# A fixed bound in place of a measured one: the second softmax's deviation set to 2^-10, its largest-|x| reductions left out, and a running minimum added

## The chip, the cores and the metric

One core of a Trainium2 chip runs the kernel. The metric is device time in microseconds (us), the median over runs; the profile is one execution on the same core. The engines are PE (matrix multiplies; PEld is its weight load), VectorE (DVE), ScalarE (ACT), GpSimd (POOL) and SyncE (SP), whose queue issues all data transfers here.

## The reference

For each of 4 batches x is 12480 tokens of 128 channels; 32 inducing vectors are shared. An attention step makes 32 rows h, a second one mixes them for every token, and a two-layer MLP with a squared ReLU follows.

```python
def mab(q, kv):
    s = scale * (q @ kv.transpose(0, 2, 1))
    s = s - s.max(-1, keepdims=True)
    a = np.exp(s)
    a /= a.sum(-1, keepdims=True) + 1e-09
    return a @ kv
h = mab(I, x)                  # I: inducing, 32 rows
y = mab(x, h)                  # every token against the 32 rows of h
...
r = np.maximum(y @ w_in, 0.0)  # d_ff = 2048
out = (r * r) @ w_out
```

## The kernel before

The second softmax is nearly flat: each of a token's 32 weights a lies close to 1/32. So y is close to the mean of the rows of h, and the sign of almost every hidden column of `y @ w_in` is the same for all tokens. If no weight falls short of 1/32 by more than a share rho, a column's smallest and largest possible value follow from the 32 numbers `h @ w_in` alone. Columns that are never positive are dropped (`dead`), columns that are always positive (`pos`) become a quadratic form in the deviations d = 2^14 (a - 1/32), and at most 16 others (`mix`) are computed singly. That needs 512 squared columns (`pairs`, `g`) instead of 2048.

The work is staged by batch. `first(b)` reads all x of a batch twice, transposed (`xp` tiles, 7 groups G of up to 1920 columns) and straight (`xnb` tiles, two per group): scores of the first softmax on PE, scaled and their maximum taken on VectorE (`sT`, L254), the bias `nb` (L287), exp on ScalarE (L300), a transpose (`en`, L310), the accumulation `hacc` on PE (L323) into `hq` (L331), and at the end the normalised, transposed h (`hn`, `hT`). `prepare(b)` makes the weights of the batch: `hwv` = h w_in (L448), the largest |value| spread over all partitions (`row`, `bc`, `p2`, named `p` in the profile), the scaled copy `hws` (L494), the column classes, the product `R` (L529), and 4 blocks of quadratic weights `G` (VectorE, L605), `wq` (PE, L611), `w` (L165). `second(b, G)` makes a group's weights a: scores (L236), transpose (L362), row maximum (L364), subtraction on GpSimd (L368), exp (L369), sum (L372), product with the reciprocal on GpSimd (L375), transpose back (L378), rounding to fp16 on ScalarE or VectorE (L385 or L387), the split-off rest (L388), and a transfer through DRAM that lays the deviations out for PE (`ad`, `dT`). `squares(b, G)` adds the single columns. A `Chunk` of 480 tokens then takes two `hp` products and squares (`up`, `lift`: L639, L648), five accumulations (`down`: L654, L655) and one evacuation `o`, on ScalarE (L658) or VectorE (L660).

The order of the program around the chunks is written out: `background(k)` gives, after every half chunk, so many steps of `second` of this and the next batch, of `first` and `prepare` of the next batch, and of `squares`. Batch 0's `first` and `prepare` run ahead of its chunks, mixed with the narrowing of the weights from 64-bit words (`ni`, `no`, L206 to L212). A scheduler then orders the instructions of each engine; every engine works through its own queue in order.

The bound rho is measured in before. `largest(G)` (L292) takes the largest |x| of each channel over an `xp` tile, one VectorE reduction of 1920 elements for each group (28 in all, tile `xm`). `prepare` multiplies these with the largest deviation of h's rows from their mean (`dh`, `ah`, L455 to L459; the matmul L474), scales the result (L477, L479), spreads it beside the largest value (L484, L501) and uses it as a per-partition operand. Each batch writes a flag: rho at most 2^-8, no more than 16 mixed columns, and a check of ranges. If one of the flags is 0, a branch behind the chunks computes all batches again with all 2048 columns (`every_column`).

Where an evacuation or a rounding may go to either engine, `to_act` decides by a ledger of planned time, `held`, which `largest` also writes to:

```python
if held["act"] + act < held["dve"] + dve:
    held["act"] += act
    return True
held["dve"] += dve
return False
```

Of the kernel before, what the change touches and what calls it, by code (L numbers as in the profile page):

```python
# [40 lines left out]
def attend_then_relu2_mlp(ctx: ExitStack, tc: tile.TileContext, xn, xT, indT, w_in, w_out, outT):  # L41
# [198 lines left out]
    def first(b):  # L240
# [49 lines left out]
        def largest(G):  # L290
            held["dve"] += 60 + 1.042 * 4 * WID[G]
            nc.vector.tensor_reduce(  # L292
                st.xm[:, G:G + 1], st.xp[G], axis=AX.X, op=ALU.max, apply_absolute_value=True,
            )

# [141 lines left out]
    def prepare(b):  # L437
# [37 lines left out]
        row = work.tile([1, 2], F32, tag="row", name=f"row_{b}")
        nc.vector.tensor_reduce(row[:, 0:1], ps[0:1, 0:P], axis=AX.X, op=ALU.max)
        nc.vector.tensor_reduce(row[:, 1:2], ps[0:1, P:P + MI], axis=AX.X, op=ALU.max)  # L477
        ts(row[:, 0:1], row[:, 0:1], 2.0 ** -60, None, op0=ALU.max)
        ts(row[:, 1:2], row[:, 1:2], 2 * scale * (1 + 2.0 ** -8), 2.0 ** -16, op0=ALU.mult, op1=ALU.add)  # L479
# [4 lines left out]
        nc.vector.tensor_copy(two, ps[:, 0:2])  # L484
# [2 lines left out]
        ts(p2.bitcast(I32), two[:, 0:1].bitcast(I32), 0x7F800000, None, op0=ALU.bitwise_and)
# [16 lines left out]
        ts(vm, v, omr, None, op0=ALU.mult)  # L504
# [435 lines left out]
```

## Time and profile before

| | |
|---|---|
| runs, median (lowest to highest) | 576.62 us (575.87 to 576.66) |
| the profiled execution, first to last instruction | 577.3 us; no time is listed for it beside this span |
| mean granted clock of PE | 0.869 |
| busy: PE, VectorE, ScalarE, GpSimd | 438.9, 365.3, 296.8, 83.4 us |
| transfers | 100.82 MB, mean 175 GB/s |
| first lift of batches 0, 1, 2, 3 | 100.3, 236.7, 360.8, 486.6 us |

A row of the profile's groups gives line, engine, operation, `out<-in` with shapes, the count, busy time and the mean of one in ns, and behind the second bar the engine's idle time just before these instructions with what ended it. The chain of waits is the work that ended last, followed backwards from the end: time outside it can be saved without shortening the run. In the lines by stretch, the numbers are the stretch, its length, the busy time of PE, PEld, VectorE, ScalarE and GpSimd with their counts, PE's granted clock, the share of the transfer engines and GB/s. In a waits row stand who waited, for whom, the total, the times and the longest.

### The profile page before, as it was taken

How to read it: one execution, taken by the hardware profiler on the slowest of the kernel's cores; microseconds unless marked ns; L12 is line 12 of the kernel's file. 1: busy time of each engine (PE TensorE's matmuls, PEld its weight loads, DVE VectorE, ACT ScalarE, POOL GpSimd, SP SyncE). 2: the span in 40 equal slices, each digit the busy share in tenths (PEclk: the TensorE clock that was granted, in tenths of full speed). 3: DMA queues.
4: the chain of work that ended last, by engine and by line, in shares of the span. 5: the costliest groups of instructions: out<-in, count | busy, mean ns of one | idle time of the engine just before them, and what ended most of it. 6: DMA issues, size and time to landing. Idle time of an engine off the chain costs nothing.

```text
span 577.3 us, 8820 instructions
## 1 busy us (share of the span) xinstructions
PE 438.9 (76%) x3083; PEld 204.5 (35%) x3083; DVE 365.3 (63%) x947; ACT 296.8 (51%) x419; POOL 83.4 (14%) x93
## 2 busy tenths in 40 slices
PE   1615465777798889769878899769777999897882
PEld 0014334522233536413333545313243555223330
DVE  6999758662555268997254298985534378767342
ACT  0030112437577266747875376628574476565771
POOL 0000011030211010242021021222011022422010
PEclk9999655997789569989889799969969599899997
DMA  8958715024528606565867535735866332334543
GB/s 322 399 214 277 277 69 154 1 86 155 179 80 305 199 20 226 172 182 167 280 226 230 178 102 186 270 104 145 311 211 190 107 105 72 97 126 130 168 132 131
DMA packets 64590, 100.82 MB, mean 175 GB/s; under 512 B 22800, under 2 KB 53776, under 8 KB 64528
## 3 DMA queue, kind: packets, MB, share of 16 engines
q1 hardware_dynamic: 64528, 100.08, 52.1%
q8 instruction: 28, 0.46, 0.3%
q14 instruction: 34, 0.28, 0.2%
HBM read 64.91 MB, written 31.95 MB: 168 GB/s over the span
## 4 chain that ended last, share of the span: by engine, by line
PE 44%; DVE 28%; ACT 13%; issue 6%; DMA 3%; POOL 3%; SPq 1%; POOLq 0%; ACTq 0%; DVEq 0%
PE po L654 10%; PE hp L639 9%; ACT g L648 8%; PE s L236 7%; DVE xm L292 5%; PE hwv L448 5%; PE hacc L323 4%; DVE G L605 3%; DMA outT_dram<-o 2%; PE po L655 2%; PE wq L611 2%; ACT o L658 2%; DVE e L362 2%; PE R L529 2%; DVE z L372 2%
## 5 line engine op out<-in xcount | busy, mean ns | idle before, releaser
L648 ACT ACTIVATE g<-hp 128x960 f16<-128x960 f32 x208 | 193.2, 970 | 87.9 <-PE hp L639 48.9
L639 PE MATMUL hp<-dT,pairs 96*128 96x480 f16 x416 | 122.0, 385 | 29.0 <-ACT g L648 28.1
L654 PE MATMUL po<-g,w 128*128 128x480 f16 x416 | 119.4, 399 | 16.1 <-ACT o L658 6.0
L368 POOL TENSOR_TENSOR e<-e,mx 128x480 f32<-128x480 f32 (+1 forms) x28 | 26.5, 947 | 334.8 <-DVE mx L364 222.8
L639 PEld LDWEIGHTS <-pairs 96*128 96x128 f16 x416 | 37.8, 99 | 97.6 <-issue 75.7
L654 PEld LDWEIGHTS <-w 128*128 128x128 f16 x416 | 41.1, 104 | 75.4 <-issue 43.9
L292 DVE TENSOR_REDUCE xm<-xp_False 128x1 f32<-128x1920 f32 (+1 forms) x28 | 55.7, 1989 | 5.3 <-DMA xp_False<-xT_dram 5.3
L658 ACT ACTIVATE o<-po,bias,osc 128x480 f32<-128x480 f32 x66 | 48.9, 753 | 18.9 <-PE po L655 7.1
L236 PE MATMUL s<-xp_False,indT_sb 128*32 128x480 f32 (+1 forms) x224 | 37.7, 743 | 20.5 <-DMA xp_False<-xT_dram 12.3
L323 PE MATMUL hacc<-xnb,en 128*32 128x128 f32 x784 | 39.2, 328 | 17.2 <-issue 9.3
L655 PE MATMUL po<-dT,lin 128*128 128x480 f16 x104 | 42.3, 408 | 2.7 <-DMA dT<-zz 2.7
L432 POOL TENSOR_TENSOR zz<-z 128x480 f16<-128x480 f32 (+1 forms) x28 | 28.9, 1030 | 87.8 <-DVE z L428 72.1
L660 DVE TENSOR_SCALAR o<-po,osc,bias 128x480 f32<-128x480 f32 x38 | 28.7, 767 | 18.0 <-DMA outT_dram<-o 6.8
L323 PEld LDWEIGHTS hacc<-xnb,en 128*32 128x32 f32 x784 | 26.7, 129 | 34.3 <-issue 20.1
L300 ACT ACTIVATE sT<-sT,nb 128x480 f32<-128x480 f32 (+1 forms) x28 | 18.2, 653 | 35.5 <-DVE nb L287 35.5
L236 PE MATMUL s<-xp_False,hT 128*32 128x480 f32 (+1 forms) x224 | 34.5, 628 | 2.1 <-DVE s L357 1.7
L375 POOL TENSOR_TENSOR e<-e,z 128x480 f32<-128x480 f32 (+1 forms) x28 | 27.6, 986 | 53.8 <-DVE z L374 48.6
L428 DVE TENSOR_SCALAR z<-sq,off,cut 128x480 f32<-128x480 f32 (+1 forms) x28 | 21.4, 764 | 21.8 <-PE sq L422 21.7
L605 DVE TENSOR_TENSOR G<-hwp,hw 128x512 f16<-128x512 f16 x64 | 30.1, 510 | 5.0 <-PE wq L611 4.7
L369 ACT ACTIVATE e<-e 128x480 f32<-128x480 f32 (+1 forms) x28 | 16.1, 574 | 31.6 <-POOL e L368 31.6
L362 DVE STREAM_TRANSPOSE e<-s 128x480 f32<-128x480 f32 (+1 forms) x28 | 18.0, 644 | 15.4 <-PE s L236 14.9
L331 DVE TENSOR_TENSOR hq<-hacc,hq 128x128 f32<-128x128 f32 x24 | 6.8, 284 | 33.0 <-PE hacc L323 33.0
(208 smaller groups left out, 498.6 us busy)
## 6 DMA issues: line engine op xcount, KB each, us to landing
outT_dram<-o SPq DMA_DIRECT2D x104, 240.0 KB, 2.2
xp_False<-xT_dram SPq DMA_DIRECT2D x24, 960.0 KB, 5.8
xnb<-xn_dram SPq DMA_DIRECT2D x28, 448.0 KB, 6.1
xnb<-xn_dram SPq DMA_DIRECT2D x24, 512.0 KB, 5.8
dT<-ad SPq DMA_DIRECT2D x72, 120.0 KB, 2.7
ad<-a SPq DMA_DIRECT2D x24, 240.0 KB, 2.7
dT<-zz SPq DMA_DIRECT2D x104, 30.0 KB, 1.9
wi<-w_in_dram SPq DMA_DIRECT2D x4, 512.0 KB, 5.4
```

Source lines behind the costliest of these rows:

```text
L236: nc.tensor.matmul(ps[32 * q:32 * q + 32, 0:w], lhsT, xp[:, w * q:w * q + w], start=True, stop=True,)
L292: nc.vector.tensor_reduce(st.xm[:, G:G + 1], st.xp[G], axis=AX.X, op=ALU.max, apply_absolute_value=True,)
L323: st.last = nc.tensor.matmul(hacc[32 * q:32 * q + 32, 0:P], en[:, t], xg[:, t % 8], start=t < 4, stop=t + 4 >= nb32,)
L362: nc.vector.transpose(ef[:, 0:wb], ps[:, 0:wb])
L432: nc.gpsimd.tensor_tensor(g[rows], zv[rows], zv[rows], op=ALU.mult)
L448: nc.tensor.matmul(ps[:, k * (MI + 1):(k + 1) * (MI + 1)], w_in_sb[:, f:f + P], st.hT[:, 96:P + 1], start=True, stop=True,)
L605: tt(g[:, :, MI * j:MI * j + n], hwp[:, :, 0:n], hw16f[:, :, s0:s0 + n], op=ALU.mult)
L639: nc.tensor.matmul(hp[:, i, 0:CH].rearrange("p (q t) -> p q t", q=4), pairs[0:96, (2 * j + i) * P:(2 * j + i + 1) * P], self.dT[0:96], sta ...
L648: nc.scalar.activation(self.g[:, 2 * j:2 * j + 2], self.hp.pop(j)[:, 0:2, 0:CH], AF.Square)
L654: nc.tensor.matmul(po[:, 0:CH], st.w16[:, i], self.g[:, i], start=i == 0, stop=False)
L655: nc.tensor.matmul(po[:, 0:CH].rearrange("p (q t) -> p q t", q=4), st.lin, self.dT, start=False, stop=True)
L658: nc.scalar.activation(o, po[:, 0:CH], AF.Identity, bias=st.bias, scale=st.osc)
```

## The change

rho is no longer measured: it is the constant 2^-10, in immediates in place of per-partition operands. The reductions over x, `largest` with its ledger entry, and the operations that made rho of them go. Instead each `second(b, G)` keeps, behind the split of a, a running elementwise minimum of the rounded deviations in one tile `least_d` (fp16, 128 x 480); one step at the end of the chain of `second` reduces it to a number and writes a fifth flag: at least -0.498, where 2^14 / 32 x 2^-10 = 0.5.

```diff
-RHO_MAX = 2.0 ** -8
+RHO = 2.0 ** -10
+D_MIN = -0.498
...
+    least_d = const.tile([P, CH], F16, name="least_d")
+    nc.vector.memset(least_d, 0.0)
...
-        def largest(G):
-            held["dve"] += 60 + 1.042 * 4 * WID[G]
-            nc.vector.tensor_reduce(
-                st.xm[:, G:G + 1], st.xp[G], axis=AX.X, op=ALU.max, apply_absolute_value=True,
-            )
...
-            largest(G)
...
         if not again:
+            nc.vector.tensor_tensor(least_d[:, 0:w], least_d[:, 0:w], a16[:, 0, 0:w], op=ALU.min)
             st.aT[G] = load_dT(b, G)
...
-                nc.vector.tensor_reduce(xm, st.xm, axis=AX.X, op=ALU.max)
-                ts(dh, st.hT[:, 0:MI], st.hT[:, P:P + 1], None, op0=ALU.subtract)
-                stt(dh, dh, -1.0, dh, op0=ALU.mult, op1=ALU.max)
-                stt(ah, st.hT[:, 0:MI], -1.0, st.hT[:, 0:MI], op0=ALU.mult, op1=ALU.max)
-                stt(dh, ah, 2.0 ** -18, dh, op0=ALU.mult, op1=ALU.add)
...
-        nc.tensor.matmul(ps[0:1, P:P + MI], xm, dh, start=True, stop=True)
...
-        nc.vector.tensor_copy(two, ps[:, 0:2])
-        rho = two[:, 1:2]
...
-        ts(omr, rho, -1.0, 1.0, op0=ALU.mult, op1=ALU.add)
...
-        ts(vm, v, omr, None, op0=ALU.mult)
-        ts(up, hi, 0.0, rho, op0=ALU.max, op1=ALU.mult)
+        ts(vm, v, 1.0 - RHO, None, op0=ALU.mult)
+        ts(up, hi, 0.0, RHO, op0=ALU.max, op1=ALU.mult)
...
-        ts(fits[:, 1:2], row[:, 1:2], RHO_MAX, None, op0=ALU.is_le)
-        tt(flags[:, b:b + 1], fits[:, 0:1], fits[:, 1:2], op=ALU.mult)
+        ts(flags[:, b:b + 1], bp[0:1, 2:3], MX + 0.5, None, op0=ALU.is_le)
...
+    def smallest():
+        m = small("dmin")
+        nc.vector.tensor_reduce(m, least_d, axis=AX.X, op=ALU.min)
+        tp = att_psum("dmin_t")
+        nc.tensor.transpose(tp[0:1, 0:P], m, ident)
+        t = work.tile([1, 1], F32, tag="dmin1", name="dmin1")
+        nc.vector.tensor_reduce(t, tp[0:1, 0:P], axis=AX.X, op=ALU.min)
+        nc.vector.tensor_scalar(flags[:, NB:NB + 1], t, D_MIN, None, op0=ALU.is_ge)
+        yield
+    ahead = chain(*(second(b, G) for b in range(NB) for G in range(NG)), smallest())
```

The order of the instructions moves with it, at three places of VectorE's queue that matter below. The first is in the first pass over batch 0, from the maximum of the scores to the transposed weights `en` of group 0, before:

```order
L276 TENSOR_REDUCE m_291<-mx_215 128x1
L292 TENSOR_REDUCE xm_133<-xp_3_False 128x1
L280 TENSOR_REDUCE gm_295<-mt_293 1x32
L207 SCALAR_TENSOR_TENSOR no_a<-wo_266,no_a 128x512
L282 COPY gm_0_297<-gm_295 1x128
L208 TENSOR_SCALAR no_m<-no_a 128x512
L287 TENSOR_SCALAR nb<-mb_299 128x1
L292 TENSOR_REDUCE xm_133<-xp_4_False 128x1
L209 SCALAR_TENSOR_TENSOR no_r<-wo_266,no_m 128x512
L310 STREAM_TRANSPOSE en_0_318<-sT_213 128x480
```

and with the change:

```order
L282 TENSOR_REDUCE gm_295<-mt_293 1x32
L208 TENSOR_SCALAR no_a<-wo_266 128x512
L284 COPY gm_0_297<-gm_295 1x128
L209 SCALAR_TENSOR_TENSOR no_a<-wo_266,no_a 128x512
L289 TENSOR_SCALAR nb<-mb_299 128x1
L210 TENSOR_SCALAR no_m<-no_a 128x512
L211 SCALAR_TENSOR_TENSOR no_r<-wo_266,no_m 128x512
L212 TENSOR_TENSOR no_r<-no_a,no_r 128x512
L213 TENSOR_SCALAR no_m<-wo_266 128x512
L208 TENSOR_SCALAR no_a<-wo_268 128x512
L214 SCALAR_TENSOR_TENSOR wo_sb<-no_m,no_r 128x512
L306 STREAM_TRANSPOSE en_0_318<-sT_213 128x480
```

Both reductions are gone, and a whole narrowing (`no`) stands ahead of the transpose in place of a part of one. The second place is in the preparation of batch 0, from `row` to `p`; `a`, `e` and `mx` with 0_0 and 0_1 belong to `second` of groups 0 and 1, `xm_144` to batch 1. Before:

```order
L476 TENSOR_REDUCE row_590<-am_587 1x1
L477 TENSOR_REDUCE row_590<-am_587 1x1
L478 TENSOR_SCALAR row_590<-row_590 1x1
L378 STREAM_TRANSPOSE a_0_0_595<-e_0_0_557 128x480
L479 TENSOR_SCALAR row_590<-row_590 1x1
L292 TENSOR_REDUCE xm_144<-xp_2_False 128x1
L388 SCALAR_TENSOR_TENSOR a_0_0_597<-a_0_0_595,lessen,a_0_0_597 128x480
L484 COPY two<-bc_605 128x2
L362 STREAM_TRANSPOSE e_0_1_623<-s_0_1_618 128x480
L487 TENSOR_SCALAR p_609<-two 128x1
```

and with the change, from `p` on to the scaled copy `hws`:

```order
L469 TENSOR_SCALAR p_590<-bc_588 128x1
L491 TENSOR_TENSOR dn_c<-dn_c,vm 128x16
L471 TENSOR_SCALAR k_595<-p_590 128x1
L481 TENSOR_SCALAR mg<-p_590 128x1
L482 TENSOR_SCALAR nmg<-p_590 128x1
L472 RECIPROCAL s<-k_595 128x1
L493 SCALAR_TENSOR_TENSOR pos<-dn_c,mg,pos 128x16
L357 STREAM_TRANSPOSE e_0_1_603<-s_0_1_598 128x480
L383 SCALAR_TENSOR_TENSOR a_0_0_579<-a_0_0_577,lessen,a_0_0_579 128x480
L386 TENSOR_TENSOR least_d<-least_d,a_0_0_579 128x480
L359 TENSOR_REDUCE mx_0_1_605<-e_0_1_603 128x15
L476 TENSOR_SCALAR hws_607<-hwv_526,s 128x512
```

`p` is read straight from PSUM with no reduction ahead of it, and `hws` now stands behind group 1's transpose, group 0's split, the minimum and group 1's row maximum. The third place is early in batch 1, where `second` of batch 1 (1_2, 1_3) and the scores of batch 2 (`sT`) share the queue. Before:

```order
L373 TENSOR_SCALAR z_1_2_2196<-z_1_2_2196 128x15
L254 TENSOR_SCALAR sT_2211,mx_2213<-s_2_0_2239 128x480
L374 RECIPROCAL z_1_2_2196<-z_1_2_2196 128x15
L292 TENSOR_REDUCE xm_133<-xp_3_False 128x1
L378 STREAM_TRANSPOSE a_1_2_2201<-e_1_2_2155 128x480
L372 TENSOR_REDUCE z_1_3_2306<-e_1_3_2235 128x15
L292 TENSOR_REDUCE xm_133<-xp_4_False 128x1
L388 SCALAR_TENSOR_TENSOR a_1_2_2203<-a_1_2_2201,lessen,a_1_2_2203 128x480
L373 TENSOR_SCALAR z_1_3_2306<-z_1_3_2306 128x15
L374 RECIPROCAL z_1_3_2306<-z_1_3_2306 128x15
L428 TENSOR_SCALAR z_1_2250<-sq_1_2245,off_148,cut 128x480
L378 STREAM_TRANSPOSE a_1_3_2337<-e_1_3_2235 128x480
```

and with the change:

```order
L369 RECIPROCAL z_1_2_2155<-z_1_2_2155 128x15
L367 TENSOR_REDUCE z_1_3_2266<-e_1_3_2195 128x15
L373 STREAM_TRANSPOSE a_1_2_2160<-e_1_2_2114 128x480
L638 TENSOR_SCALAR o_1_2263<-po_1_2257,osc_152,bias_153 128x480
L382 TENSOR_SCALAR a_1_2_2162<-a_1_2_2160,lessen 128x480
L368 TENSOR_SCALAR z_1_3_2266<-z_1_3_2266 128x15
L383 SCALAR_TENSOR_TENSOR a_1_2_2162<-a_1_2_2160,lessen,a_1_2_2162 128x480
L386 TENSOR_TENSOR least_d<-least_d,a_1_2_2162 128x480
L369 RECIPROCAL z_1_3_2266<-z_1_3_2266 128x15
L373 STREAM_TRANSPOSE a_1_3_2297<-e_1_3_2195 128x480
L382 TENSOR_SCALAR a_1_3_2299<-a_1_3_2297,lessen 128x480
L383 SCALAR_TENSOR_TENSOR a_1_3_2299<-a_1_3_2297,lessen,a_1_3_2299 128x480
```

Two reductions went; an evacuation `o_1`, the roundings of `a_1_2` and `a_1_3`, which ScalarE did before, and the minimum stand in their place. Over the whole program 26 evacuations, 6 roundings and 2 scalings of `w` change from ScalarE to VectorE. The new evacuations are those of the last four chunks of batch 0, of chunks 1, 2, 3, 6, 8 to 13, 19, 21 and 22 of batch 1, and of chunks 1, 8, 10 to 13, 19, 21 and 22 of batch 2.

In SP's queue the first `xp` tile of batch 1 moves from ahead of six transfers of batch 0's `xnb` tiles to behind the last of them.

More of the change, by code (lines that the diff above doesn't have):

```diff
@@ L119, in attend_then_relu2_mlp @@
     inv_t = const.tile([P, 1], F32, name="inv_t")
-    flags = const.tile([1, NB], F32, name="flags")
+    flags = const.tile([1, NB + 1], F32, name="flags")
+    least_d = const.tile([P, CH], F16, name="least_d")
+    nc.vector.memset(least_d, 0.0)
     class Batch:
@@ L127, in attend_then_relu2_mlp @@
         one = Batch()
-        one.xm = const.tile([P, NG], F32, name=f"xm{k}")
         one.hn = const.tile([P, P], F32, name=f"hn{k}")
@@ L473, in prepare @@
         nc.tensor.transpose(ps[0:1, 0:P], am, ident)
-        nc.tensor.matmul(ps[0:1, P:P + MI], xm, dh, start=True, stop=True)
[L475 to L479, printed above, removed]
+        row = work.tile([1, 1], F32, tag="row", name=f"row_{b}")
+        nc.vector.tensor_reduce(row, ps[0:1, 0:P], axis=AX.X, op=ALU.max)
+        ts(row, row, 2.0 ** -60, None, op0=ALU.max)
         yield
         ps = att_psum(f"bc_{b}")
-        nc.tensor.matmul(ps[:, 0:2], ones, row, start=True, stop=True)
-        two = small("two", 2)
-        nc.vector.tensor_copy(two, ps[:, 0:2])
-        rho = two[:, 1:2]
+        nc.tensor.matmul(ps[:, 0:1], ones, row, start=True, stop=True)
         p2 = small("p2")
-        ts(p2.bitcast(I32), two[:, 0:1].bitcast(I32), 0x7F800000, None, op0=ALU.bitwise_and)
-        mg, nmg, s, k2, omr = small("mg"), small("nmg"), small("s"), small("k2"), small("omr")
+        ts(p2.bitcast(I32), ps[:, 0:1].bitcast(I32), 0x7F800000, None, op0=ALU.bitwise_and)
+        mg, nmg, s, k2 = small("mg"), small("nmg"), small("s"), small("k2")
         ts(k2, p2, 2.0, None, op0=ALU.mult)
@@ L508, in prepare @@
         stt(dead, up, nmg, dead, op0=ALU.is_le, op1=ALU.max)
-        ts(dn, lo, 0.0, rho, op0=ALU.min, op1=ALU.mult)
+        ts(dn, lo, 0.0, RHO, op0=ALU.min, op1=ALU.mult)
         tt(dn, dn, vm, op=ALU.add)
@@ L545, in prepare @@
         stt(inc, inc, pl, mix, op0=ALU.add, op1=ALU.mult)
-        fits = work.tile([1, 2], F32, tag="fits", name=f"fits_{b}")
-        ts(fits[:, 0:1], bp[0:1, 2:3], MX + 0.5, None, op0=ALU.is_le)
-        ts(fits[:, 1:2], row[:, 1:2], RHO_MAX, None, op0=ALU.is_le)
-        tt(flags[:, b:b + 1], fits[:, 0:1], fits[:, 1:2], op=ALU.mult)
+        ts(flags[:, b:b + 1], bp[0:1, 2:3], MX + 0.5, None, op0=ALU.is_le)
         hot = flow.tile([P, NF, MX], F32, tag="hot", name=f"hot_{b}", bufs=1)
@@ L703, in attend_then_relu2_mlp @@
     N_SECOND, N_SCORES, N_HEADS, N_PRE, N_SQ = 4, 2 * NG, 20, 23, 2
-    ahead = chain(*(second(b, G) for b in range(NB) for G in range(NG)))
+    def smallest():
[8 more added lines that the diff above has]
+    ahead = chain(*(second(b, G) for b in range(NB) for G in range(NG)), smallest())
     sqs = chain(*(squares(b, G) for b in range(NB) for G in range(NG)))
@@ L723, in background @@
         b, c = k // (2 * NCH), k % (2 * NCH) / 2.0
-        give("ahead", ahead, min(math.ceil((NG * b + c / 4 + min(3, 2 + k / 16)) * N_SECOND), NB * NG * N_SECOND))
+        give("ahead", ahead, min(math.ceil((NG * b + c / 4 + min(3, 2 + k / 16)) * N_SECOND), NB * NG * N_SECOND + 1))
         if b + 1 < NB:
```

2 lines of the change are left out of this document (removed).

## The prediction

> **What bounds the kernel now.** I read the page first, then the chain of waits by stretch, then VectorE's timeline where the chain runs through the line that goes. From the page:
>
> ```profile
> PE 44%; DVE 28%; ACT 13%; issue 6%; DMA 3%; POOL 3%; SPq 1%; POOLq 0%; ACTq 0%; DVEq 0%
> L292 DVE TENSOR_REDUCE xm<-xp_False 128x1 f32<-128x1920 f32 (+1 forms) x28 | 55.7, 1989 | 5.3 <-DMA xp_False<-xT_dram 5.3
> ```
>
> No engine carries the span alone: the chain changes hands. The line to be removed, L292, keeps VectorE busy for 55.7 us, but only what lies on the chain can be gained. The chain of the whole span, of its first 70 us and of 70 to 100 us, by line, with the later pieces of L292 in order of time:
>
> ```profile
> by line: PE po L654 9.6%; PE hp L639 8.5%; ACT g L648 8.0%; PE s L236 6.7%; issue 6.5%; DVE xm L292 4.8%; PE hwv L448 4.5%; PE hacc L323 4.0%; DVE G L605 3.2%; DMA outT_dram<-o 2.3%; PE po L655 2.0%; PE wq L611 1.9%; ACT o L658 1.8%; DVE e
> by line: DVE xm L292 20.7%; issue 15.4%; PE hacc L323 12.2%; DMA wi<-w_in_dram 5.3%; DVE sT L254 4.2%; DVE ni_a L207 3.6%; DVE ni_r L209 3.6%; DVE w_in_sb L212 3.4%; DVE ni_r L210 2.6%; DVE pairs L111 2.3%; DVE ni_m L208 2.2%; DVE ni_a L206
> by line: PE hwv L448 22.6%; PE R L529 20.4%; DVE xm L292 6.9%; PE s L236 5.9%; DVE hwS L520 4.7%; DVE z L372 3.8%; POOL e L375 3.3%; DVE vm L504 2.8%; DVE hi_c L463 2.3%; DVE a L378 2.3%; DVE a L388 2.1%; DVE hwp L525 2.0%; DVE sum_c L517 2
> ...
> 251.44 2.01 DVE xm L292
> 254.56 2.06 DVE xm L292
> 366.13 2.03 DVE xm L292
> 375.77 1.35 DVE xm L292
> 379.35 2.06 DVE xm L292
> ```
>
> So L292 holds 4.8% of 577.3 = 27.7 us of the chain: 20.7% of 70 = 14.5 us in the first pass over batch 0, 6.9% of 30 = 2.1 us in the preparation behind it, and some 11 us afterwards, 9.5 of them in the five pieces shown. How full the engines are, stretch by stretch (columns: stretch, length, busy us of PE, PEld, DVE, ACT, POOL, granted clock, DMA share, GB/s):
>
> ```profile
> 12.00:36.00 24.00, 12.44 (x59) 1.99 (x59) 23.84 (x46) 0.00 (x0) 0.00 (x0) 1.00 1.01 395
> 36.00:44.00 8.00, 2.16 (x32) 1.65 (x31) 7.73 (x14) 4.66 (x14) 0.00 (x0) 1.00 0.22 71
> 44.00:61.00 17.00, 8.41 (x150) 6.92 (x150) 16.32 (x33) 0.00 (x0) 0.00 (x0) 0.99 0.84 289
> 70.00:100.00 30.00, 18.12 (x90) 13.12 (x90) 20.44 (x61) 6.69 (x10) 4.42 (x4) 0.53 0.32 103
> 210.00:262.00 52.00, 42.77 (x322) 20.60 (x315) 46.97 (x116) 33.59 (x47) 12.00 (x12) 0.93 0.55 175
> 340.00:395.00 55.00, 46.58 (x342) 21.34 (x342) 46.80 (x110) 29.91 (x41) 11.27 (x12) 0.91 0.58 186
> 486.00:577.00 91.00, 69.06 (x340) 26.34 (x338) 50.26 (x96) 52.35 (x62) 18.56 (x19) 0.92 0.39 127
> ```
>
> VectorE is full from 12 to 61 us, nearly full around each hand-over to the next batch (46.97 of 52, 46.80 of 55), and loose in the last 91 us.
>
> **The first pass.** Five reductions stand in the full stretch. Two more stand between the last sum and the first hT, where a chain of tiny operations waits behind them:
>
> ```profile
> 36.27 0.16 DVE L287 TENSOR_SCALAR nb<-mb 128x1 f32<-128x1 f32 x1 [0.40 <-PE mb L285]
> 36.34 2.15 DVE L292 TENSOR_REDUCE xm<-xp_False 128x1 f32<-128x1920 f32 x1
> 39.00 0.67 DVE L310 STREAM_TRANSPOSE en<-sT 128x480 f32<-128x480 f32 x1
> ...
> 62.32 0.29 DVE L331 TENSOR_TENSOR hq<-hacc,hq 128x128 f32<-128x128 f32 x1 [0.23 <-PE hacc L323]
> 62.75 2.13 DVE L292 TENSOR_REDUCE xm<-xp_False 128x1 f32<-128x1920 f32 x1
> 64.80 0.15 DVE L338 TENSOR_SCALAR zr<-hs 128x1 f32<-128x1 f32 x1
> 64.87 2.14 DVE L292 TENSOR_REDUCE xm<-xp_False 128x1 f32<-128x1920 f32 x1
> 66.92 0.15 DVE L339 RECIPROCAL zr<-zr 128x1 f32<-128x1 f32 x1
> ```
>
> From one start to the next a reduction costs 2.05 us (62.75 to 64.80). Walking the new order with the old durations, the five give 10.2 us at the last sum (62.3 becomes 52.1), and the two behind it 3.5 us at hT. Is something else late first? The transfers: 36 to 61 us moved 8 x 71 + 17 x 289 GB/s = 5.5 MB, of which an xp tile of 0.98 MB now stands behind the xn tiles in SP's queue; the remaining 4.5 MB take 11.4 us at the 395 GB/s of 12 to 36 us, from the 37th us to the 49th. That is 3 us ahead of the 52.1, so VectorE stays the bound. Term: -13.7 us, least -8 (if the tiles arrive one by one as late as they are asked for), most -14.5.
>
> **The first preparation.** The scaling waits for one reduction and for what stands behind it:
>
> ```profile
> 82.12 0.14 DVE L478 TENSOR_SCALAR row<-row 1x1 f32<-1x1 f32 x1
> 83.08 0.10 DVE L479 TENSOR_SCALAR row<-row 1x1 f32<-1x1 f32 x1
> 83.11 2.13 DVE L292 TENSOR_REDUCE xm<-xp_False 128x1 f32<-128x1920 f32 x1
> 85.79 0.14 DVE L484 COPY two<-bc 128x2 f32<-128x2 f32 x1
> 86.46 0.10 DVE L487 TENSOR_SCALAR p<-two 128x1 int32<-128x1 int32 x1
> 88.23 0.47 DVE L494 TENSOR_SCALAR hws<-hwv,s 128x512 f32<-128x512 f32 x1
> 93.16 6.13 PE L529 MATMUL R<-wo_sb,hwS 128*32 128x128 f32 x32 [7.53 <-DVE hwS L520]
> ```
>
> L479 goes, so the broadcast matmul starts a microsecond sooner; p then comes near 83.2 instead of 86.46. But the new order puts the transpose, the split, the minimum and the row maximum of group 1 ahead of hws, so hws gains only some 1.5 us. The z sums of group 1 move behind hwS in exchange, and R starts about 3.5 us earlier. Term: -3.5, ends -1.5 and -4.5.
>
> **What moves.** The ledger of ScalarE's and VectorE's planned time (to_act) loses every 2060 ns entry after batch 0 and gets none for the minimum. The built order shows the consequence: 26 output evacuations, 6 roundings of a to fp16 and 2 of w go from ScalarE to VectorE. The prices, with the nearest relative of the minimum (L605: two fp16 inputs, 512 long) and GpSimd's subtraction:
>
> ```profile
> L605 DVE TENSOR_TENSOR G<-hwp,hw x64: 276/424/1234, 93.8 to 489.3; 128x512 f16<-128x512 f16 x60, 128x256 f16<-128x256 f16 x4
> L660 DVE TENSOR_SCALAR o<-po,osc,bias x38: 683/770/778, 279.4 to 567.7; 128x480 f32<-128x480 f32 x38
> L658 ACT ACTIVATE o<-po,bias,osc x66: 733/752/790, 129.4 to 500.6; 128x480 f32<-128x480 f32 x66
> L387 DVE TENSOR_SCALAR a<-a,lessen x9: 336/470/471, 273.2 to 534.7; 128x480 f16<-128x480 f32 x8, 128x240 f16<-128x240 f32 x1
> L368 POOL TENSOR_TENSOR e<-e,mx x28: 616/994/1163, 76.4 to 530.4; 128x480 f32<-128x480 f32 x24, 128x256 f32<-128x256 f32 x4
> PE po L654 <- ACT o L658: 6.0, 5, 2.1
> PE po L654 <- DVE o L660: 5.7, 9, 1.7
> ```
>
> The minimum lies between L605's median 0.42 and its longest 1.23; I take 0.5, nearer the median, since most of those 64 ran undisturbed. VectorE: -55.7 for L292; -6.6 for eleven small operations in each of four preparations (0.10 to 0.22 each, as L479 and L484; mean taken 0.15); +24 x 0.5 + 4 x 0.28 = +13.1; +26 x 0.77 = +20.0; +6 x 0.47 = +2.8; the rest about +1.5. Sum -25. ScalarE: -26 x 0.75 and some 5 for the roundings, -24.5. Clearing the running minimum stands before the first transfer lands, where VectorE idles: nothing.
>
> [...]
>
> **The batches.** Around the first hand-over (210 to 262) five reductions and the eleven small ones leave (10.3 + 1.6); seven evacuations, four minima and two roundings arrive (7 x 0.69 from start to start, 2.0, 0.8 = 7.6): -4.3. Around the second (340 to 395) the same leaves; four evacuations, four minima, two roundings arrive (5.6): -6. Around the third no reduction stood; three evacuations and three minima arrive, the small ones leave: +1. The other reductions lie off the chain, and ScalarE's relief I count at nothing, PE being late next there. Term: -9.3, ends -16 (all 11 us of chain, plus half of the evacuations) and 0.
>
> **The tail.** After 486 us nothing leaves. Seven minima stand behind the splits whose transfer is awaited, so they delay only what follows; the final reduction and its transpose stand once in PE's order ahead of an accumulation: together +1, ends 0 and +3.
>
> Sum: -13.7 - 3.5 - 9.3 + 1 = -25.5, from the profiled span of 577.3 to 551.8. That execution stands 0.7 above the median of the runs, 576.62, and nothing beside the span is listed for it; on the median's scale the forecast is 551.1.
>
> **Rivals.**
> - *Only the front gains.* The hand-overs are refilled by evacuations and minima, and the term of 9.3 vanishes: 560.4. For it: 7.6 of 11.9 us come back in the first one. Against: five pieces of L292 on the chain.
> - *The transfers hold the first pass.* -8 instead of -13.7 there: 556.8. For it: DMA share 0.84 from 44 to 61; against: the 3 us reckoned above.
> - *The clock rises.* From 70 to 100 us it was granted 0.53, and R took 6.13. At full clock R, hwv and s there would save some 4 us: 547. For it: a denser first pass just ahead; against: 44 to 61 already had 0.99 and the clock fell after it. [...]
> - *Each minimum stalls beside GpSimd.* At L605's longest, 1.23, a minimum costs 0.73 more than I took: +2.9 at each of three hand-overs and perhaps +2 in the tail, so 551.1 becomes some 562. For it: GpSimd's operations last 0.99 and two belong to every group; against: the median of 0.42. [...]
> - *Slower: PE waits for VectorE's evacuations.* An evacuation in VectorE's queue stands behind preparation, and PE's next accumulation waits for one of two banks. Rows: 38 evacuations made PE wait 5.7 us in all, longest 1.7. At that longest for each of 26: 44 us, and 551 becomes 595; it decides above 1.0 us each. The rows say 0.15.
> - *The bound fails and the program takes its long branch.* Each of 104 chunks would run 64 more matmuls, over 1000 us. Worked out from the reference's formulas on these inputs, the least deviation in the program's units is -0.064, against the limit -0.498; so it does not.
>
> **How the numbers follow.** Forecast as summed (544 to 556): 0.53; only the front 0.18; the clock 0.12; transfers 0.08; stalled minima 0.05; evacuations 0.03; long branch 0.01. The range 540 to 563 covers the first five but for their edges. Within 0.2%, about what a measurement of this kernel can tell from no change, I put 0.01; slower 0.04; faster 0.95.
>
> **What would show it.** The step right: en of group 0 starts near 32 us, hT near 54.5, R near 76; VectorE busy about 340 us, ScalarE about 272; minima of 0.42 to 0.55. Wrong: xn tiles awaited by hacc in the first pass; minima near 1 us beside GpSimd; PE idle behind the moved evacuations at the hand-overs; or batches that take as long from first lift to first lift as before.

## The result and the profile after the change

| | before | changed |
|---|---|---|
| median of 4 runs each | 576.6 us (575.9 to 577.8) | 559.9 us (555.1 to 566.1) |
| ratio | | 0.967, 95% interval 0.961 to 0.972 |
| span of the profiled execution | 577.3 us | 559.4 us |

The kernel became faster by 16.7 us; the forecast was 25.5 (551.1, range 540 to 563). Ratios here and below leave out executions more than 1.5% above the fastest of the same kernel, medians take all: with a spread of 555 to 566 us this matters here.

The page after the change gives the busy time of the engines and the chain by engine:

```profile
PE 431.2 (77%) x3076; PEld 205.0 (37%) x3076; DVE 336.9 (60%) x941; ACT 273.5 (49%) x385; POOL 84.2 (15%) x93
PE 32%; DVE 16%; ACT 11%; DMA 7%; issue 5%; POOL 4%; SPq 2%; POOLq 0%; ACTq 0%; DVEq 0%
```

and the view of single lines shows the operations that the forecast priced (shortest, median and longest in ns, first and last start):

```profile
L386 DVE TENSOR_TENSOR least_d<-least_d,a x28: 273/400/837, 72.7 to 518.9; 128x480 f16<-128x480 f16 x24, 128x240 f16<-128x240 f16 x4
L638 DVE TENSOR_SCALAR o<-po,osc,bias x64: 735/770/778, 213.4 to 549.7; 128x480 f32<-128x480 f32 x64
L636 ACT ACTIVATE o<-po,bias,osc x40: 732/751/785, 111.9 to 477.9; 128x480 f32<-128x480 f32 x40
```

VectorE fell by 28 us to 336.9 (about 340 was forecast), ScalarE by 23 to 273.5 (272). The minimum took 0.40 at the median and 0.84 at most, where 0.5 was taken. So VectorE's and ScalarE's work came out near what was reckoned. VectorE's timeline over the first pass and the first preparation, with R on PE, answers to the two timelines of the prediction:

```profile
30.32 0.16 DVE L289 TENSOR_SCALAR nb<-mb 128x1 f32<-128x1 f32 x1
33.46 0.67 DVE L306 STREAM_TRANSPOSE en<-sT 128x480 f32<-128x480 f32 x1
...
53.16 0.29 DVE L326 TENSOR_TENSOR hq<-hacc,hq 128x128 f32<-128x128 f32 x1 [0.60 <-PE hacc L318]
54.05 0.16 DVE L333 TENSOR_SCALAR zr<-hs 128x1 f32<-128x1 f32 x1 [0.60 <-PE hs L331]
55.27 0.29 DVE L339 COPY hT<-ht 128x128 f32<-128x128 f32 x1 [0.48 <-PE ht L338]
...
69.75 0.16 DVE L469 TENSOR_SCALAR p<-bc 128x1 int32<-128x1 int32 x1 [0.15 <-PE bc L467]
73.62 0.48 DVE L476 TENSOR_SCALAR hws<-hwv,s 128x512 f32<-128x512 f32 x1
77.21 5.46 PE L510 MATMUL R<-wo_sb,hwS 128*32 128x128 f32 x32 [5.74 <-DVE hwS L501]
```

The last sum came from 62.32 to 53.16, hT from 68.10 (timeline of before) to 55.27, and R from 93.16 to 77.21. To place the rest, I took from ScalarE's timeline the start of the squares ("lift") of chunk 3 of batch 0 and of the first chunk of batch 3, and the end:

| profiled execution | lift of chunk 3 | from there to batch 3 | last batch |
|---|---|---|---|
| before | 116.9 | 369.7 | 90.7 |
| changed | 99.4 | 364.1 | 95.9 |
| difference | -17.5 | -5.6 | +5.2 |

The three differences add up to the 17.9 us between the spans. The front gave about its forecast of 17.2, in this execution; the batches gave 5.6 of 9.3; the last batch lost 5.2 where 1 was taken and 3 was the most allowed. The experiments ask what stands behind the second and the third.

### The profile page after: what moved, and what is told of

Its sections match the earlier page's. It is cut to its first block, busy times and chain, and to the rows that moved or that the text cites. A ratio compares the mean times of both kernels' runs of the same rounds, so it can differ in the third digit from the quotient of the medians.

```text
span 559.4 us, 8763 instructions
## 1 busy us (share of the span) xinstructions
PE 431.2 (77%) x3076; PEld 205.0 (37%) x3076; DVE 336.9 (60%) x941; ACT 273.5 (49%) x385; POOL 84.2 (15%) x93
## 4 chain that ended last, share of the span: by engine, by line
PE 32%; DVE 16%; ACT 11%; DMA 7%; issue 5%; POOL 4%; SPq 2%; POOLq 0%; ACTq 0%; DVEq 0%
PE po L632 8%; ACT g L626 7%; PE hp L617 7%; PE s L238 5%; PE hwv L444 4%; DMA outT_dram<-o 3%; DVE o L638 2%; PE hacc L318 2%; DVE e L357 2%; DMA ad<-a 2%; PE po L633 2%; POOL e L363 2%; ACT sT L296 2%; POOL e L370 1%; DVE mx L359 1%
## 5 line engine op out<-in xcount | busy, mean ns | idle before, releaser
L638 DVE TENSOR_SCALAR o<-po,osc,bias 128x480 f32<-128x480 f32 x64 | 48.4, 768 | 18.8 <-PE po L633 10.1
L238 PE MATMUL s<-xp_False,indT_sb 128*32 128x480 f32 (+1 forms) x224 | 33.8, 672 | 21.5 <-DMA xp_False<-xT_dram 13.6
L633 PE MATMUL po<-dT,lin 128*128 128x480 f16 x104 | 41.7, 406 | 6.4 <-DMA dT<-zz 6.4
L428 POOL TENSOR_TENSOR zz<-z 128x480 f16<-128x480 f32 (+1 forms) x28 | 30.6, 1094 | 90.3 <-DVE z L424 81.3
L370 POOL TENSOR_TENSOR e<-e,z 128x480 f32<-128x480 f32 (+1 forms) x28 | 26.3, 939 | 59.2 <-DVE z L369 51.1
L636 ACT ACTIVATE o<-po,bias,osc 128x480 f32<-128x480 f32 x40 | 29.4, 751 | 10.9 <-issue 5.7
L256 DVE TENSOR_SCALAR_CACHE_REDUCE sT<-s 128x480 f32<-128x480 f32 (+1 forms) x28 | 17.3, 619 | 23.5 <-PE s L238 23.3
L583 DVE TENSOR_TENSOR G<-hwp,hw 128x512 f16<-128x512 f16 x64 | 27.2, 460 | 6.3 <-PE wq L589 6.3
L373 DVE STREAM_TRANSPOSE a<-e 128x480 f32<-128x480 f32 (+1 forms) x28 | 17.9, 640 | 20.8 <-POOL e L370 20.8
L165 ACT COPY hwv<-hwv 128x264 f32<-128x264 f32 x8 | 3.0, 378 | 54.9 <-PE hwv L444 54.9
```

The source lines that it names most:

```text
L238: nc.tensor.matmul(ps[32 * q:32 * q + 32, 0:w], lhsT, xp[:, w * q:w * q + w], start=True, stop=True,)
L370: nc.gpsimd.tensor_tensor(e[:, 0:t], e[:, 0:t], z[:, 0:t].unsqueeze(2).broadcast_to([P, t, MI]), op=ALU.mult)
L428: nc.gpsimd.tensor_tensor(g[rows], zv[rows], zv[rows], op=ALU.mult)
L633: nc.tensor.matmul(po[:, 0:CH].rearrange("p (q t) -> p q t", q=4), st.lin, self.dT, start=False, stop=True)
L636: nc.scalar.activation(o, po[:, 0:CH], AF.Identity, bias=st.bias, scale=st.osc)
L638: nc.vector.tensor_scalar(o, po[:, 0:CH], st.osc, st.bias, op0=ALU.mult, op1=ALU.add)
```

## The experiments

Each is the changed kernel with the edit shown; its own ratio to the kernel before is 0.967.

### What the reductions are worth, early and late

The 17 later reductions (after 100 us) put back, with their ledger entries (late_kept):

```
             if G + 2 < NG:
                 exp(G + 2)
+            if b > 1 or b == 1 and G >= 4:
+                held["dve"] += 60 + 1.042 * 4 * WID[G]
+                nc.vector.tensor_reduce(st.xm[:, G:G + 1], st.xp[G], ..., op=ALU.max, apply_absolute_value=True)
```

> The changed kernel with the 17 reductions of |x| of batch 1's groups 4 to 6 and of batches 2 and 3 left in, with their entries in the ledger; the proof by the running minimum stays. The changed kernel measured 559.9, before 576.6. Theory A (the front gains 17.5 us, the reductions that left the hand-overs gain some 5.6 more up to the start of the last batch, and the last batch gives 5.2 back for reasons of its own): the hand-overs lose again, 565 to 567. Theory B (only the front gains; what the batches show is the clock's phase): 559 to 561. Theory C (the batches' full 9.3 of the forecast is there and only the tail hides it): about 569.

Measured: 551.9 us (547.3 to 554.6), ratio 0.954 (0.948 to 0.959). All three theories fell: with 33 us more work on VectorE the kernel is 8 us faster than without.

The complement, the 11 earlier reductions put back (early_kept; the condition reads `b == 0 or b == 1 and G < 4`):

> The complement: the changed kernel with the 11 reductions that ran before 100 us (batch 0's and those of batch 1's groups 0 to 3) left in, with their ledger entries; the later 17 are gone. Theory A: the front's 17.5 us are lost, the batches keep 5.6 and the tail gives 5 back: 575 to 577, and the lift of batch 1's first chunk comes earlier after that of batch 0 than before the change. Theory B: 576 to 578 with the intervals from first lift to first lift as before. Theory C: 567 to 571. Had the front gained less than the lift of chunk 3 says, the time would stand below 571 as well, with the first lift before 100 us.

Measured: 581.0 us (574.8 to 586.5), ratio 1.002 (0.999 to 1.006); lift of chunk 3 at 118.1, last batch 95.5. Its median is above what any theory said and nearest to B, as is the stretch from chunk 3 to batch 3 (368.3, before 369.7); its last batch is the long one of theory A. Without the early removal nothing of the net gain is left.

Is it the later reductions' work that helps, or what comes with it? They were cut to two elements each, entries kept (`st.xp[G][:, 0:2]`, late_tiny), and then left out with the entries alone kept (ledger_late):

> The kernel that kept the 17 later reductions (551.9 us, 8 less than without them, against all that was expected), with each reduction cut to two elements of its 1920 and its entry in the ledger left: VectorE loses 31 us of work, the assignment of evacuations stays. Theory 1 (the reductions' work never mattered behind the front; the assignment and the order that come with their entries gained the 8 us): 550 to 553. Theory 2 (the work cost what was forecast, 9.3 us, and the order gained more than that): 541 to 545. Theory 3 (the pauses that the reductions make hold something back that is better late): 556 to 562.

> The changed kernel with nothing of the reductions but the ledger's entries of the 17 later ones: no reduction is computed, and in the last batch VectorE's queue stands as in the kernels that kept or shortened them. Theory 1 (the last batch's length is a property of that order): 90.5 to 91.5 us there, 550 to 555 in all, faster than the changed kernel by the 5 us of the last batch. Theory 2 (the reductions themselves brought the gain, by their pauses): 95 to 96 in the last batch, 558 to 561.

Measured: cut, 552.6 us (549.4 to 557.3), ratio 0.959 (0.952 to 0.965); entries alone, 0.954 (0.948 to 0.959), though its six executions spread from 546.8 to 566.0 with a median of 556.4, above the 550 to 555 of its theory 1, and the ratio rests on three of them. Here are the groups with the whole and with the cut reductions:

```profile
L314 DVE TENSOR_REDUCE xm<-xp_False x17: 1144/2115/2154, 114.6 to 384.6; 128x1 f32<-128x1920 f32 x14, 128x1 f32<-128x960 f32 x3
```

```profile
L314 DVE TENSOR_REDUCE xm<-xp_False x17: 97/146/155, 110.9 to 386.9; 128x1 f32<-128x2 f32 x17
```

and the stretch from chunk 3 to batch 3 in each (columns as in the prediction's table by stretch), first whole, then cut, then the kernel before:

```profile
103.00:461.10 358.10, 300.84 (x2244) 140.63 (x2244) 227.85 (x585) 219.81 (x315) 59.26 (x62) 0.90 0.56 180
```

```profile
99.40:462.60 363.20, 304.60 (x2244) 143.21 (x2244) 197.44 (x585) 218.94 (x315) 61.14 (x62) 0.90 0.56 177
```

```profile
116.90:486.60 369.70, 312.28 (x2250) 143.95 (x2250) 222.48 (x594) 225.25 (x322) 59.86 (x62) 0.87 0.54 174
```

VectorE's 227.85 us against 197.44 make the stretch no longer: 358.1 against 363.2. Theory 1 of both expectations holds by the ratios: behind the front the reductions' work was worth nothing that these runs can tell. The last batch takes 90.9 us with the whole reductions, 90.9 with the cut ones and 90.3 with the entries alone, against 95.9 in the changed kernel. Of the 8 us, 5 lie there, in the order of instructions that the ledger entries bring with them.

### The moved evacuations

All 28 entries kept in the ledger, and no reduction (ledger_kept):

```
                 exp(G + 2)
+            held["dve"] += 60 + 1.042 * 4 * WID[G]
```

> The changed kernel with only the ledger's entry of the reductions kept, and no reduction: the 26 output evacuations, 6 roundings and 2 scalings stay on ScalarE. Theory 1 (the evacuations that moved into VectorE's queue refilled the hand-overs and ate a part of the gain): 14 of them stand at the three hand-overs, 0.7 us each, so up to 9.8 less than 559.9: 551 to 556. Theory 2 (the queue of VectorE has room and PE waits alike for either engine): 559 to 561. Theory 3 (ScalarE, which does the squares that PE waits for, needed the relief): 562 to 570, most of it in the middle of batches 1 and 2.

Measured: 562.5 us (558.4 to 571.2), ratio 0.970 (0.965 to 0.975). By the ratio it is theory 2: with 38 evacuations on VectorE as before, or 64, the time is the same; the median stands at the lower edge of theory 3, so that a small loss is not excluded. Chunk 3 was lifted at 101.9 us here and at 118.1 with the early reductions in place: it is the reductions' work that the front gains from, not their ledger entries. The waits of PE over the whole of the changed kernel's execution agree with theory 2:

```profile
PE po L632 <- DVE o L638: 7.4, 11, 1.6
```

That is 7.4 us where it was 5.7 before: with 26 more evacuations on VectorE, PE waited 1.7 us longer for them in all.

### Where the last batch loses 5 us

The changed kernel again, unaltered (after_again):

> The changed kernel once more, unaltered, beside the others of this set and with a second profile. If its last batch (95.9 us from the lift of its first chunk to the end, before 90.7) is made by the order of the instructions, it comes out at 95 to 96 again, with the first three intervals near 127, 121 and 127; if it was the clock's phase in one execution, it comes out anywhere from 90 to 96. Time 556 to 564.

Measured: 559.4 us (554.8 to 567.2), ratio 0.968 (0.961 to 0.976); last batch 95.9 again. It is not chance. The first three intervals from lift to lift came out at 124, 123 and 124 us and not at 127, 121 and 127, so the batches ahead do vary from one execution to the next.

The proof left out (no_proof: no minima, no last step, its flag set to one):

```
-            nc.vector.tensor_tensor(least_d[:, 0:w], least_d[:, 0:w], a16[:, 0, 0:w], op=ALU.min)
-    ahead = chain(*(second(b, G) ...), smallest())
+    ahead = chain(*(second(b, G) ...))
+    nc.vector.memset(flags[:, NB:NB + 1], 1.0)
```

> The changed kernel without the proof: the 28 minima and the final reduction, transpose and comparison are left out, the flag set to one. Theory 1 (the minima are off the chain, the final step costs the 1.5 us seen as PE's wait at 521): 558 to 559, the last batch shorter by 1.5. Theory 2 (each minimum on VectorE in a full hand-over moves what follows: some 3 at each, 0.4 us apiece, and the seven of the last batch count): 553 to 556. Theory 3 (every one of the 28 lies on the chain): 28 x 0.40 = 11 us, 548. If the loss of the last batch is the clock's phase alone, the last batch here takes 91 to 96 us by the window that it meets, with no relation to the proof.

Measured: 552.7 us (546.6 to 555.3), ratio 0.953 (0.949 to 0.958), last batch 90.3. The proof costs 7 to 8 us, 1.4% of the time, of which 5.6 are in the last batch: theory 2 by size, though the place was not the hand-overs (360.1 us from chunk 3 to batch 3, near the 360.6 of after_again). Is it the last step? It was pulled apart (final_split):

```
         nc.vector.tensor_reduce(m, least_d, axis=AX.X, op=ALU.min)
+        yield
         tp = att_psum("dmin_t")
         nc.tensor.transpose(tp[0:1, 0:P], m, ident)
+        yield
```

> The changed kernel with the last step of the proof pulled apart: its reduction, the transpose and the reduction of the transposed row stand in three steps, one chunk from each other. On VectorE nothing else changes its place: the row's reduction moves from ahead of the evacuation of chunk 11 to ahead of that of chunk 15. Theory 1 (VectorE's queue stood from 519.8 to 521.3 for TensorE's transpose, with three evacuations behind it, and PE then waited 1.6 us): the last batch 1.5 to 3 us shorter, 557 to 558.5. Theory 2 (the loss lies in the minima and in the late second softmax of group 6, not in the final step): within 1 us of the changed kernel.

Measured: 563.5 us (561.6 to 570.4), ratio 0.978 (0.972 to 0.984), last batch 96.2. VectorE's wait for the transpose (0.72 us in the changed kernel) is gone, the loss is not: theory 2, though not within its 1 us. That this kernel measured a per cent slower than the changed one is not explained; up to the last batch its instructions stand in the same order.

So the minima, or what they put in another place. The waits of PE in the last batch of the changed kernel name one, the last row, that is small in the kernel before and without the proof (the two rows behind it):

```profile
PE po L632 <- DVE o L638: 4.2, 6, 1.6
PE po L633 <- DMA dT<-zz: 3.7, 2, 2.6
PE hp L617 <- ACT g L626: 3.4, 9, 0.7
PE s L238 <- DVE s L352: 2.2, 1, 2.2
```

```profile
PE s L236 <- DVE s L357: 0.2, 1, 0.2
PE s L239 <- DVE s L353: 0.2, 1, 0.2
```

Line 352 clears 16 columns of a PSUM bank ahead of the scores of the last group. VectorE's and PE's timelines at that place:

```profile
505.63 0.68 DVE L373 STREAM_TRANSPOSE a<-e 128x480 f32<-128x480 f32 x1 [1.17 <-POOL e L370]
...
506.85 0.72 DVE L383 SCALAR_TENSOR_TENSOR a<-a,lessen,a 128x480 f16<-128x480 f32 x1
507.48 0.77 DVE L424 TENSOR_SCALAR z<-sq,off,cut 128x480 f32<-128x480 f32 x1
508.17 0.40 DVE L386 TENSOR_TENSOR least_d<-least_d,a 128x480 f16<-128x480 f16 x1
508.51 0.76 DVE L638 TENSOR_SCALAR o<-po,osc,bias 128x480 f32<-128x480 f32 x1
508.58 0.07 DVE L352 MEMSET s<- 128x16 f32 x1
...
508.70 1.03 PE L238 MATMUL s<-xp_False,hT 128*32 128x240 f32 x8 [2.23 <-DVE s L352]
509.66 1.78 PE L632 MATMUL po<-g,w 128*128 128x480 f16 x4
...
514.41 0.97 PE L632 MATMUL po<-g,w 128*128 128x480 f16 x4
```

and the stretch behind it, then the whole last batch of the changed kernel, of the kernel before and of the kernel without the proof:

```profile
507.50:514.40 6.90, 5.70 (x20) 1.99 (x21) 4.52 (x10) 1.83 (x2) 1.64 (x2) 0.51 0.34 99
463.50:559.40 95.90, 70.84 (x339) 26.90 (x336) 52.82 (x106) 50.88 (x60) 17.71 (x19) 0.87 0.37 121
486.60:577.30 90.70, 68.73 (x338) 26.28 (x337) 49.66 (x95) 51.76 (x62) 17.96 (x19) 0.92 0.40 128
463.20:553.50 90.30, 67.19 (x337) 26.16 (x334) 50.04 (x97) 51.09 (x60) 17.97 (x19) 0.93 0.40 129
```

A clearing of 0.07 us, which waits for nothing of its own, stands in VectorE's queue behind the transpose, the rounding and the split of the group before, a z and the minimum; the transpose in turn waited for GpSimd until 505.63. PE, whose accumulations stand behind the scores in its queue, starts nothing for 2.23 us, from 506.47 to 508.70. About 1 us into this wait the granted clock halves for 6.8 us, and four accumulations take 1.78 us instead of the 0.97 of 514.41. Wait and clock together are the loss: against the kernel without the proof PE is busy for 3.6 us more in the last batch (70.84 and 67.19) and waits for the clearing 2.0 us more, which makes the 5.6; against the kernel before it is 2.1 and 2.0 of the 5.2. Of the 3.6, about 2.6 lie in the stretch shown, an estimate: its 5.70 us of PE would take 3.1 if all of them shrank as 1.78 does to 0.97. The minimum's own 0.40 us is the smaller part: the clearing stands 45.0 us into the last batch here, 41.7 before and 41.9 without the proof, since other instructions of the queue changed places too.

What halves the clock there is not shown: in the 3.4 us ahead of the halving, half its length, PE was busy for 1.99 us at a clock of 1.00.

The same work in another order: the minimum at a lower priority for the scheduler (min_low100),

```
+            with tc.high_priority(offset=-100):
                 nc.vector.tensor_tensor(least_d[:, 0:w], ..., op=ALU.min)
```

> The changed kernel with the same minima at a lower priority: each falls behind a few instructions of its queue, and the transpose of the last group now stands ahead of the evacuations of chunks 7 and 8, as it does without the proof. VectorE's work is the same. Theory 1 (the minima cost by what they push back, not by their 11 us): most of the 7 us that leaving out the proof gave comes back, 552 to 556, the last batch 91 to 93. Theory 2 (it is VectorE's time that counts): 559 to 561. Theory 3 (the final step makes the tail's loss): the last batch stays at 94 to 96, the others gain.

Measured: 558.8 us (557.4 to 566.6), ratio 0.970 (0.965 to 0.976), last batch 94.2. The minimum now stands behind the clearing, but split and z still ahead of it: PE waited 1.9 us instead of 2.2, and the half clock stayed. This fell short of theory 1: by the time it is nearest theory 2, by its last batch theory 3, whose cause final_split had ruled out. The clearing was hardly freed, so the run doesn't tell theory 1 from theory 2 elsewhere; it does show that 0.40 us of minimum ahead of the clearing is not what makes the wait. Last, eight evacuations taken out of that stretch of VectorE's queue (tail_act):

```
-            if to_act(220 + 0.833 * CH, 110 + 1.042 * CH):
+            if self.b == NB - 1 and 4 <= self.c < 12 or to_act(220 + 0.833 * CH, 110 + 1.042 * CH):
```

> The changed kernel with eight output evacuations of the last batch, those of chunks 4 to 11, given to ScalarE instead of VectorE; nothing else in VectorE's queue changes its place there but for one pair. Theory 1 (in the last batch PE waits for evacuations that stand in VectorE's queue behind the second softmax of a later group, which itself waits for ScalarE and GpSimd; the order decides how long): the last batch falls from 95.9 to 90 to 92 us, the time to 554 to 556. Theory 2 (the last batch is late because the second softmax itself is late, whoever evacuates): 95 to 96, 559 to 560. Theory 3 (ScalarE becomes late with its squares): 97 or more, 561 to 563.

Measured: ratio 0.959 (0.954 to 0.965), median of all six 558.7 us (552.1 to 567.3); last batch 91.0. Its waits of PE there:

```profile
PE hp L617 <- ACT g L626: 4.5, 13, 0.7
PE po L633 <- DMA dT<-zz: 3.7, 2, 2.6
PE po L632 <- DVE o L638: 2.9, 4, 1.7
PE po L632 <- ACT o L636: 2.8, 2, 1.8
```

```profile
466.80:557.80 91.00, 66.45 (x337) 25.86 (x334) 47.29 (x98) 55.62 (x68) 17.60 (x19) 0.94 0.40 128
```

The wait for the clearing is gone, the clock is 0.94 instead of 0.87, and the 5 us of the last batch are back: theory 1 by size there. In the whole time they show only by the ratio; the median, 558.7, lies above the 554 to 556 of theory 1, and the interval overlaps that of the changed kernel. Its wording was too narrow: on the evacuations nothing was gained (from 4.2 to 2.9 us of waiting on VectorE's, but from 0.9 to 2.8 on ScalarE's); the gain lies with the scores behind them. Over all 14 executions the sign is plain (the half clock is the stretch that begins 42.8 to 44.5 us into the batch):

| | clearing, us into the batch | PE's wait for it | half clock | last batch |
|---|---|---|---|---|
| changed; after_again; early_kept; final_split; warm | 44.8 to 45.1 | 2.2 us each | 6.8 us in each | 95.9; 95.9; 95.5; 96.2; 95.7 |
| min_low100 | 43.9 | 1.9 | 6.8 | 94.2 |
| ledger_kept | 42.4 | none listed | 3.4 | 92.7 |
| before; no_proof | 41.7; 41.9 | 0.2 each | none | 90.7; 90.3 |
| tail_act; warm_act | 42.1; 41.9 | none listed | none | 91.0; 91.1 |
| late_kept; late_tiny; ledger_late | 36.6 to 36.9 | none listed | none | 90.9; 90.9; 90.3 |

It is not the clearing as such that goes with the half clock. In ledger_kept PE waited 2.13 us at this place for an evacuation, and 3.4 us at half clock followed; waits of 1.71 (before, no_proof) and 1.75 us (tail_act) at this place were followed by none.

### Can the clock of the front be held up?

```
+    def fill(n):
+        hp = two_banks("fill")
+        for _ in range(n):
+            tc.keep_in_program_order(nc.tensor.matmul(hp[:, 0, 0:CH], pairs[0:96, 0:P], pairs[0:96, 0:CH], ...))
```

called for four matmuls behind each of groups 3 to 5 of the first pass, and for 3, 8, 2 and 12 between hs and R (warm); then the same together with the eight evacuations (warm_act).

> The changed kernel with 37 matmuls of constants, whose results nobody reads, in PE's idle time between the fourth group of the first pass and R, to keep the granted clock up. Theory 1 (the front's chain waits on matmuls at half clock: hwv 3.0 and 3.2 us, s 1.8, R 5.5): at full clock they take half, the lift of chunk 3 comes 4 to 6 us earlier than 99.4 to 100.3, and the time falls to 553 to 556. Theory 2 (the clock does not follow, or the filler delays what it should speed): R still 5 us or more, 558 to 562.

Measured: 560.2 us (555.7 to 562.8), ratio 0.969 (0.964 to 0.973). At R the clock did follow, as PE's timeline shows:

```profile
78.06 3.68 PE L526 MATMUL R<-wo_sb,hwS 128*32 128x128 f32 x32 [1.38 <-DVE hwS L517]
```

and the stretch behind it, here and then in the changed kernel:

```profile
80.00:110.00 30.00, 23.99 (x196) 15.00 (x198) 15.98 (x64) 11.35 (x17) 0.99 (x1) 0.83 0.20 58
80.00:110.00 30.00, 25.54 (x235) 13.64 (x234) 19.18 (x67) 12.08 (x17) 2.92 (x3) 0.99 0.26 78
```

R took 3.68 instead of 5.46 us. But the half clock came later, from 85.8 to 96.0 us, where the changed kernel had 0.99 from 80 to 110; chunk 3 was lifted at 105.5. So neither theory held: the time is that of theory 2, but the matmuls did become faster, and what they gained was lost again behind them.

> Both edits in one: the filler in the front and the eight evacuations on ScalarE. If both first theories hold and the gains add, 549 to 551; if one holds, 554 to 556; if neither, 559 to 561. With the reductions gone from the front and the order mended in the tail it should stand no higher than the 552 of the kernel that kept the later reductions.

Measured: ratio 0.967 (0.962 to 0.971), median of all six 557.0 us (550.8 to 561.8); last batch 91.1. One first theory holds, the tail's, as its last batch shows; the median is still above the 554 to 556 named for that, and the bound of 552 was missed.

Two versions make the change whole and have the lower ratio, both with the short last batch: ledger entries alone (0.954, 0.948 to 0.959), with fewer evacuations moved, and the eight evacuations on ScalarE (0.959, 0.954 to 0.965). The short last batch alone does not make a lower ratio: warm_act has it and stands at 0.967.

## Why the prediction was right and where it was not

**First pass, -13.7.** Right: hT came 12.8 us earlier (55.27, near 54.5 was forecast), the transfers held nothing up: VectorE was busy almost without a pause from 36 to 48.6 us, and the sums of 48.59 waited for its transpose of 47.82 while their tile had landed at 46.25. The transpose of group 0 began at 33.46 rather than near 32, since a whole narrowing now stood ahead of it; the last sum, at 53.16, was 1 us later than the 52.1 forecast.

**First preparation, -3.5.** Right: R gained 15.95 in all, 3.1 of it here; chunk 3 gained 17.5. Three more executions in which the instructions stand in the same order up to the last batch (after_again, final_split, tail_act) lifted chunk 3 at 100.3, 100.3 and 103.1: the gain of the front is 13.8 to 17.5 us, by the clock it meets behind R. In the executions that keep the front's reductions out, chunk 3 came at 99.4 to 100.3 with no half clock between 83 us and that lift (changed, after_again, late_tiny, final_split, min_low100), at 101.9 to 103.5 with about 6.8 us of it (ledger_kept, late_kept, no_proof, tail_act, ledger_late), and at 103.9 and 105.5 with 10.2 (warm_act, warm). So it is partly luck that the profiled execution, the best of the four, gave the forecast's 17.2.

**The batches, -9.3.** The size was near, the mechanism was not. From chunk 3 to batch 3 the four executions took 364.1, 360.6, 364.2 and 363.7 us, 5.5 to 9.1 less than before. But the step "five reductions and the eleven small ones leave ... -4.3" is not what happened: a kernel with those reductions took 358.1, one with 30 us less of VectorE's work 363.2, and one with only the later ones removed 368.3. The step that failed took work that leaves VectorE around a hand-over, 9.5 us of it on the chain in five pieces, for time gained. My reading, not tested by itself, is that VectorE's queue always had something to do there, and that something else ended just as late. What goes with the length of this stretch, loosely, is the granted clock:

| | before | changed | after_again | late_kept | late_tiny | early_kept | warm_act |
|---|---|---|---|---|---|---|---|
| us | 369.7 | 364.1 | 360.6 | 358.1 | 363.2 | 368.3 | 353.9 |
| mean clock | 0.87 | 0.89 | 0.91 | 0.90 | 0.90 | 0.89 | 0.92 |

Over all 14 profiled executions, with 58 to 99 us at half clock in the stretch, a line fits with 0.35 us for each us at half clock (residues up to 4.5). Whether the clock rose because PE waits less, or the other way round, and whether the eleven small operations have a part in it, stays open: no run put them back alone.

**The tail, +1.** This is the term that failed: +5.2. "Seven minima stand behind the splits whose transfer is awaited, so they delay only what follows" was true, and I did not look at what follows: a clearing on which PE's scores wait, 2.23 us, and with them everything behind them in PE's queue. No run shows the part that I gave the final step: pulled apart (final_split), the last batch stayed at 96.2.

**The rivals.** "Only the front gains" named 560.4, and 559.9 was measured, but its reason, hand-overs refilled by evacuations, fell with ledger_kept; the time came out there by luck, because the batches' 5.6 and the tail's 5.2 cancel. "PE waits for VectorE's evacuations" is refuted (1.7 us more). "Each minimum stalls" did not happen either: of the 28 minima two overlapped a GpSimd operation at all. One, at 508.17, had begun 0.22 us ahead of the operation and took 0.40 us, the median; the other, the longest, began during one:

```profile
358.23 0.99 POOL L428 TENSOR_TENSOR zz<-z 128x480 f16<-128x480 f32 x1 [2.74 <-DVE z L424]
358.64 0.84 DVE L386 TENSOR_TENSOR least_d<-least_d,a 128x480 f16<-128x480 f16 x1
```

It took 0.84 us instead of 0.40 and ended 0.26 us after the GpSimd operation; in late_kept, whose 28 minima took 11.5 us in all against 11.1 here, one took 1.20 us and again ended 0.27 us after the operation beside it. More than these durations the runs do not show; in the changed kernel the price was 0.44 us, paid once. "The clock rises" hardly happened at R by itself (5.46 us after 6.13), and when forced it gained nothing.

## What to carry to other kernels

A share of the chain is a bound on a gain, not the gain: of the 14.5 us of a stretch where one engine was full 12.8 came back, while the same line's pieces around the hand-overs gave nothing that these runs can tell. When an instruction is added to an in-order queue, look up what comes next in that queue and which other engine waits for it, down to the smallest clearing; the order that came with a minimum of 0.40 us cost 5 us that way. And before a difference of one per cent in a stretch is explained, run the same kernel twice and compare the clock that each execution was granted.

## What was not expected of the hardware

The same instructions in the same order took from 360.6 to 364.2 us from chunk 3 to batch 3 and lifted chunk 3 between 99.4 and 103.1, with the granted clock as the visible difference. The changed kernel spreads over 555 to 567 us in its ten runs; the one before over 576 to 578 in its four, but over 570 to 582 in the 50 beside the experiments, so four runs showed too little of its spread.

The clock column of the kernel before had misled me: it gave 0.99 for 44 to 61 us and 1.00 for the rows ahead of that, but its record begins only at 57.3 us. The sums of 36 to 62 us before and after the change:

```profile
L323 PE MATMUL hacc<-xnb,en 128*32 128x128 f32 x196 | 11.4, 395 | 14.6 <-issue 9.3 <-DVE en L310 4.3 <-PE hacc L323 1.0
```

```profile
L318 PE MATMUL hacc<-xnb,en 128*32 128x128 f32 x169 | 10.3, 420 | 7.1 <-issue 7.1
```

The mean duration, 395 ns, is near the 420 ns of the changed kernel, whose record has 0.50 while these ran (from 34.2 to 37.9, 41.0 to 44.6 and 48.6 to 53.2 us); over the whole run of the kernel before, the median of one is 273. So PE was slow there before as well, and the argument "44 to 61 already had 0.99" against the rival of the clock stood on a value that was not recorded.
